# Two more feature groups through the seven-product scheme, early block products, fewer transposes on the matrix engine, and the last rows sent directly

## The chip, the cores and the metric

The kernel runs on one core of a Trainium2 chip. A core has five engines with their own instruction queues: PE (matrix products into PSUM, eight banks of 128 x 512 f32), DVE and ACT (both read PSUM; DVE adds, ACT applies functions such as Mish), POOL and SP. POOL, SP and ACT also issue DMAs, which all share the core's 16 DMA engines. Every queue is in order: an instruction that waits holds up what stands behind it on its engine.

The metric is the device time of one execution in microseconds (us). Three runs of the kernel before gave 936.93, 937.04 and 938.18, a median of 937.04.

## The reference

The network has four layers over `x` of 2048 tokens by 1024 channels (bf16), A B A B, each added to its input:

```
def _A_ref(x, w_r, w_i):
    X = rfft2(x.astype(float32)) * (w_r + 1j * w_i)
    return irfft2(X, s=(S, D)).astype(bfloat16)

def _B_ref(x, w1, b1, w2):
    h = einsum("bsd,df->bsf", x, w1) + b1
    act = h * tanh(softplus(h))               # Mish
    return einsum("bsf,fd->bsd", act, w2)

x = x + _A_ref(_layernorm(x), ...)
x = x + _B_ref(_layernorm(x), ...)            # and both once more
```

`w1` is 1024 x 3584 and `w2` 3584 x 1024. Both A layers use the same filter, both B layers the same weights.

## The kernel before, in words

**Layer A** computes the transforms as matrix products in stages (`s1`, `s2`, `s3`, the filter, `i1`, `i2`, `i4`). `s1` reads a rearranged copy `XR` of the normalized rows. For the second A layer `XR` is filled from the end of the first B layer, as described below.

**Layer B** works on 2048 tokens as two passes of 1024, each pass as two chunks of 512 tokens. The normalized rows of chunk c are held transposed in `XT[c]`, eight blocks of 128 channels by 512 tokens. The 3584 features are 14 groups of 256 (two tiles of 128).

For a pass, the first product `x w1` can be done in two ways for each feature group:

- *plain* (`mm1`, L1134): for each chunk, 2 feature tiles x 8 matrix products, so 32 products of 128x128 by 128x512 for the group. A chunk's product needs nothing of the other chunk. Three PSUM banks rotate; ACT applies Mish straight from PSUM.
- *seven products* (`quads`, L1178): Strassen's scheme in Winograd's form over a 2 x 2 split (two feature tiles and two halves of the channels on the side of the weights; two halves of the channels and two chunks on the side of the tokens). A group takes 7 products of 4 matrix products each, 28 in all, with sums of weight blocks (S1 to S4, four POOL instructions per group, L1081, on the first use; afterwards they are read back from a scratch tensor in DRAM) and sums of token blocks (T1 to T4 on DVE, L1163: three by the first call of `token_sums`, T3 by the second, which overwrites a part of `XT` and so comes after the last plain product of chunk 1). The block product A11·B11 is copied out of PSUM by ACT (L574) as P1, because several outputs need it, and the bank is then also accumulated further by A12·B21. DVE adds the parts (L1191, five per group), and ACT applies Mish.

In the order before, in each layer's first pass, groups 0 to 5 are plain and 6 to 13 go through the seven products. In the second pass all 14 do. The first pass of each layer begins under a filling-up phase: the last product of layer A (`i4`, called from `rest`), the residuals, the layernorm statistics (four tiles' sums on ACT, L453) and the transposes of chunk 1 run while PE does plain products of chunk 0. Its order on PE is: groups 0 to 3 of chunk 0 in halves, groups 4 and 5 of chunk 0 with the transposes of chunk 1's first two tiles inside group 5, then chunk 1 (groups 0 and 1 in halves, with the other two transposed tiles inside, then 2 to 5), then `quads`. The order on ACT around groups 4 and 5 is: Mish of group 2, two statistics instructions of tile 6 (L453), Mish of group 3, two of tile 7, then Mish of groups 4 and 5. The weight sums of the first four seven-product groups wait on POOL for a gate, namely the DVE instruction that normalizes tile 7. All weight loads go out through SP.

`products` (L1276) is the second product with `w2`, also in a seven-product scheme, with seven stages n of four token tiles t; `extra(n, t)` is other work put between. In pass 1's `products`, tiles 12 to 15 of the next pass are normalized at (1, 3). Tile 12 is turned by 8 DMA transposes issued one by one from SP (`normal`, `turn`), tiles 13 to 15 by 8 PE transposes each at (2, 2) with an ACT copy out of PSUM (`transposed`, L1100).

In the last `products` of the first B layer, each finished tile j is normalized and brought into `XR`, as rows: tiles up to 14 by a store to a DRAM scratch (`xn_store`, POOL) and a load from it one step later (`xr_load`, SP), tile 15 by 16 direct transfers from its buffer (`xr_direct`, 16 KB each, over POOL, ACT and SP). PE meanwhile repeats 24 products whose result nobody reads (`spin`, L650), and then waits for `XR`.

Of the kernel before, what the change touches and what calls it, by code (L numbers as in the profile page):

```python
# [180 lines left out]
class KB:  # L181
# [513 lines left out]
    def layer_A(self, li):  # L695
# [254 lines left out]
        self.w1_buf = [self.alloc(f"W1_{i}", (self.ob["WS"] + i * 4096, 140 * K)[i > 4], [8, 256]) for i in range(6)]  # L950
        for fg in range(6):
            self.load_w1(self.w1_buf[fg].ap, fg, [self.w1_buf[fg].res], after=self.r_ut)
# [118 lines left out]
    def fill_slot(self, b, fg, after=()):  # L1071
# [5 lines left out]
        self.load_w1(b.raw, fg, [b.res])  # L1077
        A = lambda n: self.wblock(b, n)
# [6 lines left out]
    def layer_B(self, li, last):  # L1085
# [92 lines left out]
        def quads(fgs, slot_of, B, after, lead=None):  # L1178

            sums = open_sums()  # L1180

            def product(n, bank, a, b, start):
# [5 lines left out]
                            for db in range(4)], reads=[s.res, s.rs] + list(res), writes=[self.r_bank[bank]])  # L1188
# [9 lines left out]

            def parts(n):
                a, b, d = (3 * (n % 2) + i for i in range(3))  # L1200
                return a, b, d, sums[n % 2], sums[2 + n % 2], sums[4], 2 * fgs[n]

            N = len(fgs)
            for n in range(N + 1):
                if n < N:
                    a, b, d, p1, u2, u3, ft = parts(n)
                    product(n, a, "A11", "B11", True)
                    self.copy(act, p1.ap, PS[:, a, :], [self.r_bank[a]], [p1.res])
                    product(n, b, "S2", "T2", True)
                    add(u2, b, p1)  # L1210
                if n == N and lead:
                    lead()
                if n:
                    _, pb, pd, q1, q2, q3, pft = parts(n - 1)
                    mish(1, pft + 1, q3.ap, q3.res)
                    product(n - 1, pb, "A22", "T4", False)
                    add(q1, pb, q1)
                    mish(0, pft + 1, q1.ap, q1.res)
                    product(n - 1, pd, "S4", "B22", False)
                    add(q2, pd, q2)  # L1220
                    mish(1, pft, q2.ap, q2.res)
                    after(n - 1)
                if n < N:
                    product(n, d, "S1", "T1", True)
                    product(n, a, "A12", "B21", False)
                    mish(0, ft, PS[:, a, :], self.r_bank[a])
                    product(n, b, "S3", "T3", False)
                    add(u3, b, p1)
                    add(u3, d, u3)
# [203 lines left out]
        assert self.u0 == P  # L1433
        for j in range(4, 8):
            residual(j)
# [9 lines left out]
        mm1(0, 4)  # L1445
        at_tiles(1)
        mm1(0, 5, mid=turns(1, 0, 1))
# [6 lines left out]
        early = self.open_slots("WE", self.ob["W2"], 0, 1, 2, 3)  # L1454
        for n in range(4):
            self.fill_slot(early[n], 6 + n, [gate])
# [9 lines left out]
        ws = []  # L1466
        for fg in range(2, 6):
            if fg in (2, 4, 5):
                ws += self.open_slots("WS", self.ob["WS"], len(ws))
                self.fill_slot(ws[-1], 9 + len(ws))  # L1470
            mm1(1, fg)
            if fg == 2:
                token_sums(0, last=False)
            if fg == 3:
                for j in range(8, 12):
                    residual(j)
        order = early + ws + early[:1]
        B = token_sums(0)
        self.xn_buf = self.xn_out + [self.alloc(f"XN{i}", self.ob["XN2"] + i * 2048, [self.D]) for i in range(2)]

        def after(n):
            if n == 0:
                self.fill_slot(order[7], 13)
            if 1 <= n < 4:
                load_b(STD, n // 3, (n - 1) % 2)
            if n < 4:
                self.stats_dve(8 + n)
            if n == 4:
                self.scales(8, 4)
            if n > 3:  # L1490
# [158 lines left out]
```

## Time and profile before

| what | value |
|---|---|
| median of three runs | 937.04 us |
| the profiled execution, its own time | 936.66 us |
| its span, first to last instruction | 934.9 us |
| PE busy | 875.9 us, 94% of the span |
| DVE, ACT, POOL busy | 619.1, 427.5, 159.0 us |
| mean granted PE clock | 0.987 |
| `mm1` (L1148) | 576 matrix products |
| `quads` (L1186) | 1232 matrix products |
| `products` (L1268) | 1568 matrix products |

PE is busy nearly everywhere, but a busy PE is modelled and a matrix product's duration (379 ns for 512 columns) contains a latency that overlaps with the next one. What one more product costs is read from a run of them without a wait: in the chain of work, 216 products of L1186 take 46.62 us, so 0.2158 us each; a product of 256 columns takes 0.109 us (16 in 1.75 us), a 128-column transpose 0.056 us (24 in 1.34 us).

### The profile page before, as it was taken

The numbers are of one execution on the slowest core, as the hardware profiler recorded it, in microseconds if no ns is written. First come the engines' busy times: TensorE is split into PE (matmuls) and PEld (weight loads), VectorE is DVE, ScalarE is ACT, GpSimd is POOL, SyncE is SP. The second block draws the span as 40 slices with busy tenths as digits, with TensorE's granted clock in tenths as the row PEclk, the third lists the DMA queues.
The fourth block names the chain that finished last, engine by engine and source line by source line (L and its number), as shares of the span: only waits on it lengthen the run. The fifth ranks groups of instructions, "written<-read, shape, count | busy, mean of one in ns | idle before, by whom it ended". The sixth has DMA issues, their size and how long they took to land.

```text
span 934.9 us, 13481 instructions
## 1 busy us (share of the span) xinstructions
PE 875.9 (94%) x5473; PEld 471.7 (50%) x5473; DVE 619.1 (66%) x973; ACT 427.5 (46%) x623; POOL 159.0 (17%) x183
## 2 busy tenths in 40 slices
PE   0799799999999999999979987999999999999998
PEld 0577486444444444444437765754444444444443
DVE  7698468686889667568746865647746665554473
ACT  7798485456203485510008975745551015552000
POOL 4922004950005642000130200000000000000000
PEclk9999999999999999999999997999999999999999
DMA  9969854676895488274640797433255635832432
GB/s 288 265 227 300 204 151 131 216 249 171 268 274 196 164 314 296 91 261 142 241 133 32 227 228 196 158 118 119 54 190 175 207 113 193 279 118 78 171 127 110
DMA packets 146335, 174.68 MB, mean 187 GB/s; under 512 B 66248, under 2 KB 125736, under 8 KB 146152
## 3 DMA queue, kind: packets, MB, share of 16 engines
q1 hardware_dynamic: 133424, 127.48, 44.5%
q0 software_dynamic: 10672, 44.67, 13.4%
q10 hardware_dynamic: 2176, 1.66, 0.6%
q8 instruction: 43, 0.70, 0.3%
q14 instruction: 20, 0.16, 0.0%
HBM read 130.00 MB, written 40.89 MB: 183 GB/s over the span
## 4 chain that ended last, share of the span: by engine, by line
PE 83%; DMA 5%; DVE 5%; ACT 2%; SPq 2%; POOL 1%; issue 1%; DVEq 0%; ACTq 0%; POOLq 0%
PE PS L1268 35%; PE PS L1186 28%; PE PS L1148 9%; SPq L251 2%; PE PS L799 2%; PE PS L725 2%; PE PS L824 2%; PE PS L1020 2%; POOL ARENA L1081 1%; PE PS L1109 1%; DMA ARENA<-in_A_x_dram 1%; DMA ARENA<-c_bt 1%; DMA ARENA<-u_scratch 1%; DMA u_scratch<-ARENA 1%; PE PS L635 1%; ACT ARENA L641 1%
## 5 line engine op out<-in xcount | busy, mean ns | idle before, releaser
L1268 PE MATMUL PS<-ARENA 128*128 128x512 bf16 x1568 | 340.1, 379 | 0.0
L1186 PE MATMUL PS<-ARENA 128*128 128x512 f16 (+1 forms) x1232 | 267.8, 379 | 0.4 <-POOL ARENA L1081 0.3
L1268 PEld LDWEIGHTS PS<-ARENA 128*128 128x128 bf16 x1568 | 153.4, 98 | 184.5
L1191 DVE TENSOR_TENSOR ARENA<-PS,ARENA 128x512 f32<-128x512 f32 x220 | 151.7, 691 | 95.7 <-PE PS L1186 90.7
L1186 PEld LDWEIGHTS PS<-ARENA 128*128 128x128 bf16 x1232 | 120.1, 98 | 146.8 <-POOL ARENA L1081 2.2
L1196 ACT ACTIVATE ARENA<-ARENA,B 128x512 bf16<-128x512 f32 x132 | 95.1, 721 | 66.5 <-DVE ARENA L1191 60.6
L574 ACT ACTIVATE ARENA<-PS 128x512 f32<-128x512 f32 (+2 forms) x82 | 61.1, 745 | 119.1 <-PE PS L1186 96.4
L1148 PE MATMUL PS<-ARENA 128*128 128x256 bf16 (+1 forms) x576 | 86.7, 308 | 0.3
L1081 POOL TENSOR_TENSOR ARENA<-ARENA 128x512 bf16<-128x512 bf16 x56 | 71.4, 1274 | 72.6 <-DVE ARENA L524 58.3
L453 ACT ACTIVATE ARENA<-XS 128x1024 bf16<-128x1024 bf16 x52 | 54.8, 1053 | 36.5 <-DVE XS L1319 33.0
L1148 PEld LDWEIGHTS PS<-ARENA 128*128 128x128 bf16 x576 | 55.2, 98 | 26.7 <-DVE ARENA L1114 1.0
L1293 DVE TENSOR_TENSOR ARENA<-ARENA 128x3584 bf16<-128x3584 bf16 x32 | 63.9, 2018 | 0.0
L1319 DVE TENSOR_TENSOR XS<-PS,ARENA 128x512 bf16<-128x512 f32 x52 | 35.7, 690 | 38.9 <-PE PS L1268 38.7
L1152 ACT ACTIVATE ARENA<-PS,B 128x256 bf16<-128x256 f32 (+1 forms) x72 | 38.3, 542 | 35.3 <-PE PS L1148 34.8
L1311 DVE TENSOR_TENSOR ARENA<-PS,ARENA 128x512 f32<-128x512 f32 x48 | 32.9, 688 | 28.9 <-PE PS L1268 28.4
L1196 ACT ACTIVATE ARENA<-PS,B 128x512 bf16<-128x512 f32 x44 | 30.2, 686 | 18.0 <-PE PS L1186 18.0
L1307 DVE TENSOR_TENSOR ARENA<-ARENA,XS 128x512 f32<-128x512 f32 x52 | 36.7, 731 | 0.5
L1163 DVE TENSOR_TENSOR ARENA<-ARENA 128x2048 f16<-128x2048 bf16 x16 | 25.3, 1582 | 17.6 <-PE PS L1148 17.3
L799 PE MATMUL PS<-ARENA 128*128 128x256 bf16 x256 | 32.4, 273 | 3.9 <-DVE ARENA L788 3.2
L472 DVE BATCH_NORM_STATS2 BN<-XS 128x6 f32<-128x512 bf16 x52 | 32.6, 669 | 4.5 <-DMA XS<-in_A_x_dram 4.5
L444 ACT ACTIVATE RS<-MV,EPS 128x1 f32<-128x1 f32 (+2 forms) x11 | 3.3, 296 | 70.7 <-DVE MV L565 70.0
L777 ACT ACTIVATE ARENA<-PS 128x1024 bf16<-128x1024 f32 x32 | 33.3, 1071 | 4.5 <-PE PS L773 4.5
(97 smaller groups left out, 820.9 us busy)
## 6 DMA issues: line engine op xcount, KB each, us to landing
ARENA<-in_B_w_dram SPq DMA_DIRECT2D x30, 896.0 KB, 6.4
ARENA<-w1s_scratch SPq DMA_DIRECT2D x30, 896.0 KB, 4.7
ARENA<-w2s_scratch SPq DMA_DIRECT2D x24, 896.0 KB, 6.7
ARENA<-in_B_w_dram SPq DMA_DIRECT2D x26, 512.0 KB, 5.2
w1s_scratch<-ARENA POOLq DMA_DIRECT2D x14, 896.0 KB, 4.2
u_scratch<-ARENA SPq DMA_DIRECT2D x14, 512.0 KB, 3.5
ARENA<-u_scratch SPq DMA_DIRECT2D x14, 512.0 KB, 5.9
w2s_scratch<-ARENA POOLq DMA_DIRECT2D x8, 896.0 KB, 4.1
```

Of the source, the lines that this page charges most:

```text
L453: self.op(act, lambda e, i=i, f=f: e.activation(junk.ap, x, f, accum_out=sums[:, i:i + 1]), reads=[self.r_xs[j]], writes=[junk.res], parts ...
L574: fn = (lambda e: e.activation(dst, src, ACT.Copy)) if scale is None else \
L799: fns.append(lambda e, c=c, part=part: e.matmul(ps[:, c * 256:(c + 1) * 256], yk.ap[:, part, c * P:(c + 1) * P], t[:, (128, 0)[part]:(384, ...
L1081: self.op(self.pool, lambda e, dst=A(dst), x=A(x), y=A(y), op=op: e.tensor_tensor(dst, x, y, op), reads=[b.res] + list(after), writes=[b.rs])
L1148: fns.append(lambda e, db=db, bank=bank, fl=fl: e.matmul(PS[:, bank, 0:w], wb.ap[:, db, fl * P:(fl + 1) * P], x.ap[:, db, tok], start=(db ...
L1152: self.op(act, lambda e, bank=bank, ft=ft, at=at: e.activation(at[:, tok], PS[:, bank, 0:w], ACT.Mish, bias=self.B1[:, ft:ft + 1]), reads= ...
L1186: self.group([lambda e, db=db: e.matmul(PS[:, bank, :], A[:, db, :], mov[:, db, :], start=(start and db == 0), stop=(db == 3), skip_group_ ...
L1191: self.op(dve, lambda e: e.tensor_tensor(dst.ap, PS[:, bank, :], x.ap, ALU.add), reads=[self.r_bank[bank], x.res], writes=[dst.res])
L1196: self.op(act, lambda e: e.activation(at, src, ACT.Mish, bias=self.B1[:, ft:ft + 1]), reads=[res, self.r_b1], writes=[ra])
L1268: self.group([lambda e, i=i, k=k, b=PB[n][k].ap: e.matmul(PS[:, bank, :], ap[:, i, t * P:(t + 1) * P], b[:, i - 7 * k, :], start=(start an ...
L1293: self.op(dve, lambda e: e.tensor_tensor(ap[dst][:, f, :], ap[x][:, f, :], ap[y][:, f, :], op), reads=part(x, k) + part(y, k), writes=part ...
L1307: self.op(dve, lambda e: e.tensor_tensor(a[t], a[t], x, ALU.add), reads=[rx], writes=[r[t]])
```

## The change

Six things change; the first four are in the first pass of each B layer.

1. Groups 4 and 5 move from plain to the seven products: plain are 0 to 3, and `quads` runs over ten groups, 4 to 13. Only four plain weight buffers remain.
2. `quads` is split. `first(n)` does the two products of group n that read chunk 0 only (A11·B11 with the ACT copy of P1, then A12·B21 with its Mish). It is called for the first four groups where plain groups 4 and 5 of chunk 0 stood: three times before the transposes of chunk 1's first two tiles, once after. `run` then leaves these two products out for the first four groups. Two more P1 buffers are given, so that four stand at once.
3. The loads of those groups' raw weights (`fill_raw`) are issued earlier than their sums (`fill_sums`), and a product waits for the sums only if it reads one. The gate stays where it was.
4. The loads, statistics, scales and normalizations that `after(n)` issues are moved to other values of n; two more slots are refilled within the run.
5. At (1, 3) of the first `products`, tiles 12 and 13 (in the last layer 12, 13 and 14) go by DMA transposes, and only 14 and 15 (15) by PE.
6. At the end of the first B layer, tiles 13 and 14 go by `xr_direct` too (8 transfers each, alternating between POOL and SP; tile 12 is loaded in the step of tile 13), tile 15's 16 transfers are dealt out to ACT, POOL, SP as 6, 6 and 4, and `spin` repeats 38 products instead of 24.

The core of the diff:

```
-        for fg in range(6):
+        for fg in range(4):
             self.load_w1(self.w1_buf[fg].ap, fg, ...)
...
+    def fill_raw(self, b, fg):
+        r = self.r_w1d[fg]
+        if r.writes:
+            self.dma(self.sp, b.ap[:, 0:2048], self.w1s_d[fg][:, 0:2048], ..., writes=[b.res])
+        else:
+            self.load_w1(b.raw, fg, [b.res])
...
-                            for db in range(4)], reads=[s.res, s.rs] + list(res), ...
+                            for db in range(4)], reads=[s.res] + [s.rs] * (a[0] == "S") + list(res), ...
...
+            def block(n):
+                a, b, d, p1, u2, u3, ft = parts(n)
+                product(n, a, "A11", "B11", True)
+                self.copy(act, p1.ap, PS[:, a, :], [self.r_bank[a]], [p1.res])
+            def corner(n):
+                a, b, d, p1, u2, u3, ft = parts(n)
+                product(n, a, "A12", "B21", False)
+                mish(0, ft, PS[:, a, :], self.r_bank[a])
+            def first(n):
+                block(n)
+                corner(n)
...
-        mm1(0, 4)
         at_tiles(1)
-        mm1(0, 5, mid=turns(1, 0, 1))
+        first, run = quads(list(range(4, 14)), order, B, (102 * 1024, self.ob["XN2"]))
+        for n in range(3):
+            first(n)
+        for f in turns(1, 0, 1):
+            f()
+        first(3)
...
-        for fg in range(2, 6):
+        for fg in (2, 3, 4, 5):
...
-                normal(12)
-                for j in (13, 14, 15):
+                for j in range(12, by_pe):
+                    normal(j)
+                for j in range(by_pe, 16):
                     xn[j] = self.apply(j)
...
-                if j < 15:
+                if j < 13:
                     self.xn_store(j, b)
-                if j > 8:
-                    self.xr_load(j - 1)
-                if j == 15:
-                    self.xr_direct(j, b, 2, (pool, act, sp))
+                    if j > 8:
+                        self.xr_load(j - 1)
+                elif j < 15:
+                    self.xr_direct(j, b, 1, (pool, sp))
+                    if j == 13:
+                        self.xr_load(12)
+                else:
+                    self.xr_direct(j, b, 2, (act, pool, sp, act, pool, act, pool, sp) * 2)
...
-            self.spin(24, 7)
+            self.spin(38, 7)
```

## The prediction

> **What bounds the kernel now.** I read the page first: PE is busy for 94% of the span, so I looked for where PE would wait afterwards. The chain of waits, in the first layer B (columns: start, length, what, all us), shows PE running without a hole through the place that is rebuilt:
>
> ```profile
> 137.08 10.42 PE PS L1148 x72
> 147.50 0.89 PE PS L1109 x16
> 148.39 4.35 PE PS L1148 x32
> 153.22 1.30 DVE ARENA L1114 x2
> 154.57 17.48 PE PS L1148 x96
> 172.05 46.62 PE PS L1186 x216
> ...
> 481.85 6.10 DMA ARENA<-ARENA
> 488.19 5.29 PE PS L635 x48
> ```
>
> So every product taken away is worth its 0.216 us (46.62 / 216), and every new wait on PE costs its full length. The last two lines are the hand-over to the second layer A: there a direct row transfer ends the wait.
>
> The timeline of the other engines around it tells what PE will wait for:
>
> ```profile
> 143.21 0.82 ACT L1152 ACTIVATE ARENA<-PS,B 128x256 bf16<-128x256 f32 x2
> 145.10 1.06 ACT L453 ACTIVATE ARENA<-XS 128x1024 bf16<-128x1024 bf16 x1
> 146.15 2.08 ACT L1152 ACTIVATE ARENA<-PS,B 128x512 bf16<-128x512 f32 x3
> 154.55 5.55 DVE L1163 TENSOR_TENSOR ARENA<-ARENA 128x2048 f16<-128x2048 bf16 x3
> 160.03 6.32 DVE L1396 TENSOR_TENSOR XS<-XS,ARENA 128x1024 bf16<-128x1024 bf16 x4
> 166.68 4.85 POOL L1081 TENSOR_TENSOR ARENA<-ARENA 128x512 bf16<-128x512 bf16 x4
> 172.16 2.50 DVE L1163 TENSOR_TENSOR ARENA<-ARENA 128x2048 f16<-128x2048 bf16 x1 [5.82 <-PE PS L1148]
> 172.95 0.60 ACT L574 ACTIVATE ARENA<-PS 128x512 f32<-128x512 f32 x1 [0.17 <-PE PS L1186]
> ```
>
> ACT is late here: group 4's Mish, ready on PE at about 144, begins at 146.15, after tile 7's statistics (L453). DVE has 5.82 us to spare before T3, the last L1163.
>
> **The change part by part** (durations from the one profiled execution, 936.66 us with a span of 934.9; the median shown is 0.38 above it).
>
> *Fewer products.* Two groups go from 32 to 28 products in each layer: 16 x 0.216 = -3.45 us.
>
> *The early products wait for ACT.* Before, PE filled three banks in turn and went on while ACT lagged. Now A12·B21 goes into the bank that ACT must first have copied as P1, directly behind A11·B11 and with nothing between them. Group 4's A11·B11 takes bank 0, whose last Mish (group 3) ends at 144.03; so it ends at about 145.0. Its copy stands behind tile 7's statistics and runs from 146.15 to 146.75. From ACT to PE I take 0.15 us (the last L641 copy ends at 500.03, L725 starts at 500.18), so A12·B21 ends at 147.76. Each further group costs 0.86 + 0.04 + 0.60 + 0.15 + 0.86 = 2.51 us instead of 1.73; Mish of the one runs under the A11·B11 of the next. Groups 5 and 6 end at 152.8, the transposes (1.00 with their gap) at 153.8, group 7 at 156.3. Before, the same point was 148.39 + 8 x 0.216 = 150.12: +6.2 us. DVE's scales and normalizations hang on the transposes and move with them, and so do the next transposes; only 0.1 of PE's 0.34 us wait ahead of 154.57 is absorbed: +6.1 us in each layer, +12.2 in all. With no hand-over time it would be +5.5 a layer; those are the bounds 11.0 and 12.4.
>
> *Raw weights.* Landings before: 141.3 for the first, 143.1 for the second, and the transfers' burst ends by 147. Needed are they at 144.1, 147.8, 150.3 and 153.8. Nothing; if the cover were gone, the wait would be one landing, 5 us.
>
> *T3 comes too late in the first layer.* DVE does T1, T2, T4 (5.55 us), four residuals (6.32) and T3 (2.50) in a row, 14.4 us from 154.55. PE, with plain groups 4 and 5 of chunk 1 gone, starts `run` 10.4 us after 154.57 (32 products of 256 columns at 0.109 and 32 of 512) and needs T3 after two products, at 12.1. Then DVE must add u2 first (0.69) before S3·T3 may enter that bank: 14.4 + 0.7 - 12.1 = 2.9 us of wait. In the second layer POOL is idle and the same rows are short (3.74, 2.49, 1.23 us); T3 waits for the plain product itself, and 0.3 is left. Sum +3.2 (bounds 0.5 and 3.9: a T3 as short as the second layer's, or one that waits another hand-over of every kind).
>
> *POOL's sums.* They follow the gate, which moves by 5 us. A group takes 4.86 + 0.87 = 5.73 us on POOL (5.9 to 6.6 beside DVE's work). From 157.5 on, groups 5 to 10 are ready at 170.6, 177, 183, 188.6, 194.3, 200.1. PE, starting at 171.1 and held by T3, asks for them at 176.5, 181, 185, 190, 196, 202. Nothing, with only 2 us to spare; the wait for T3 is the cover. In the second pass two fewer groups are summed there, and A11·B11 need not wait for sums: the 0.34 us wait at 311.0 goes, -0.3.
>
> *DVE, ACT and slots in the run.* The first four groups take 4.3 us of PE each, five DVE adds 3.5, three Mishes on ACT 2.2; statistics (1.5) come from the third on. It fits; uncovered, one statistics pair would cost PE 0.5. The four sums' loads of the second layer are four more SP issues, ahead of nothing that is due within 10 us. Refills of slots are needed over 12 us after they are issued.
>
> *Transposes.* 24 fewer on PE: 8 in the first layer, 16 in the second, 24 x 0.056 = -1.34. Of the 24 tile blocks each now stands on SP's queue as a DMA transpose at 1.27 us (16 took 20.38), two per step of 3 us, done by stage 4; T sums at (5, 3) are 12 us later, and the weight loads behind them had as much. Nothing; uncovered, 8 of them would cost 10 us.
>
> *The hand-over.* SP's direct transfers of tile 15 started at 481.27, since SP was held by the load of tile 14, which waits for its store (476.99 + 3.62). Now SP holds no load at that time; of tiles 13 and 14 it and POOL issue four pieces each, 2.6 and 2.2 us (0.64 and 0.54 apiece) in steps of 3.02, and SP tile 12's load, whose store lands by 475.5. Tile 15 is normalized at 479.35 as before; the first half's last issue is the third of ACT or POOL, about 480.8 (ACT 0.70, POOL 0.54 apiece). Landings of 16 KB took 2.1 to 6.1 us, so 483 to 487; `spin` ends at 476.5 + 8.2 = 484.7 at the earliest. I take a start of 485.7 against 488.19, -2.5 (bounds -3.4 and -1.1). Further, the clock: before, PE idle from 481.7 to 488.2 came back at half clock, visible in the windows (last columns PEclk, DMA, GB/s):
>
> ```profile
> 486.50:487.00 0.50, 0.00 (x0) 0.00 (x0) 0.00 (x0) 0.00 (x0) 0.00 (x0) 0.56 0.22 62
> 493.00:493.50 0.50, 0.50 (x9) 0.50 (x7) 0.50 (x1) 0.00 (x0) 0.00 (x0) 0.62 0.00 0
> ...
> 567.00:568.00 1.00, 0.31 (x13) 0.34 (x14) 0.00 (x0) 0.00 (x0) 0.00 (x0) 1.00 0.64 144
> 568.00:568.50 0.50, 0.50 (x26) 0.50 (x22) 0.00 (x0) 0.00 (x0) 0.00 (x0) 0.98 0.64 144
> 568.50:569.00 0.50, 0.15 (x6) 0.04 (x2) 0.00 (x0) 0.32 (x1) 0.00 (x0) 0.50 0.64 142
> ```
>
> With 1 us of idling it stays up. `s1` then is bound by its 16 copies (ACT 1.02 to 0.93, DVE 1.23), which end 9.9 us after its start instead of 11.99: -2.0 (bounds 0 and -2.4). Together -4.5.
>
> [...]
>
> *The clock in the new holes.* PE now idles about 1.9 us twice at 142 to 147 and, in the first layer, 2.9 at T3. The lines at 566 to 568.5 show the clock halved after only 1.7 us of idling with little around it. A halved stretch lasted 6.7 to 10.1 us. At half clock an early group takes 4.25 us rather than 2.51, so a stretch costs 2.7 at least; bounds 0 and 3 places x 2.7 = 8. I take half of one, +1.4. [...]
>
> Sum: -3.45 + 12.2 + 3.2 - 0.3 - 1.34 - 4.5 + 1.4 = +7.2; 936.66 + 7.2 = 943.9. I say **944.0**.
>
> **The rivals.**
>
> - *The waits fall into slack* (faster). Place: 142 to 156, price 12.2. For it: DVE and POOL have idle time there; against it: PE has none. If the holes cost below 2.6 us a layer instead of 6.1, the change gains; with none, 936.66 - 6.4 = 930.3 (no clock loss). Chance 0.06.
> - *They are partly hidden* (half of the early waits and of T3): about 936 to 939. Chance 0.08.
> - *The clock falls in several of the holes*: without the clock's term the sum is 942.5, and 2 or 3 x 2.7 make it 948 to 950.5. For it the lines at 568; against it those at 554 to 558, with PE busy by half and the clock up. Chance 0.15.
> - *The direct rows do not come earlier*: POOL and SP now carry 16 more issues, and tile 15's transfers could stand behind tile 14's. Without the 4.5: 948.4. For it the landings of 6.1; against it the DMA engines, 0.14 to 0.65 busy in most of those us. Chance 0.13.
> - *POOL becomes the bound of the first layer's run*: were every group to take 7.4 us as the first does (6.57 + 0.87), group 9's sums would come at 201 for 196: +5, 949. Chance 0.06.
>
> **How the numbers follow.** The forecast's own case, 941 to 946.5, has a chance of 0.52. The range 939.5 to 949.5 leaves out the faster case, the partly hidden one and the upper end of the clock case. About 0.2% (1.9 us) is what a measurement tells from no change. Faster: 0.06 and a small share of the partly hidden, 0.07; the same: 0.07; slower: 0.86.
>
> **What would show it.** In the profile after, PE waits at the early products' line for ACT's L574, once about 1.9 us and three times 0.7 to 0.8 in each layer, and once about 2.9 us for DVE's first add behind T3, in the first layer only. The first product of the run comes 10.4 us after the second pair of transposed tiles. The 128-column transposes fall by 24, `spin` runs to 484.7 after shifting, L635 starts within 1.5 us of it at full clock, and `s1` takes 10 us. I am wrong if ACT's copy of P1 does not hold PE, or if the hand-over gains much more than 5 us.

## The result, and the profile after

The changed kernel takes 963.56 us (median of four runs, 960.72 to 964.71) beside 937.61 for the kernel before: a ratio of 1.0272, with a 95% interval from 1.0246 to 1.0298. The forecast was 944.0 with a range up to 949.5; the sign was right, and the size too small by a factor of nearly four. The profiled execution took 964.36 us with a span of 962.6, against 936.66 and 934.9: 27.7 us more (26.0 between the medians).

Both programs go through the same stages on PE, so the difference can be laid out by the start of each stage's first product (from the timeline of PE in both traces; the last column is what the forecast's terms make of it):

| stage on PE, us | before | after | difference | forecast |
|---|---|---|---|---|
| start to the last `i4` of the first layer pair | 136.92 | 139.25 | +2.3 | 0 |
| from there to chunk 1's first product, first pair | 13.04 | 20.93 | +7.9 | +6.1 (and the clock, 1.4 in all) |
| on to `products` (rest of the plain groups, the run) | 68.55 | 75.72 | +7.2 | +1.2 |
| `products` of the first pass | 87.67 | 92.42 | +4.8 | -0.4 |
| seven-product groups of the second pass | 83.86 | 82.96 | -0.9 | -0.3 |
| last `products`, hand-over, up to `s1` | 98.15 | 98.70 | +0.5 | -2.5 |
| `s1` to `i4` of the second pair | 79.50 | 78.70 | -0.8 | -2.0 |
| second pair: to chunk 1's first product | 13.04 | 20.90 | +7.9 | +6.1 |
| second pair: on to `products` | 68.55 | 67.55 | -1.0 | -1.4 |
| second pair: `products` of the first pass | 87.68 | 87.56 | -0.1 | -0.9 |

The three stages that are left out (the second pair's last `i4`, second pass and last `products`) add up to 0.0. In the first row the two kernels differ in weight loads alone. In the 14 executions profiled for this study this point was reached between 136.9 and 140.4 us, and the six of them that keep the old form of the first layer up to there span that whole range; so the 2.3 lie within the variation from one execution to the next.

Who waited for whom on PE in the changed kernel (total us, times, longest):

```profile
PE PS L1208 <- ACT ARENA L574: 7.5, 8, 1.7
PE PS L1208 <- DVE ARENA L1213: 5.3, 3, 3.1
PE PS L635 <- DMA ARENA<-ARENA: 4.0, 1, 4.0
PE PS L1208 <- ACT ARENA L1173: 4.0, 2, 2.0
PE PS L1307 <- DMA ARENA<-in_B_w_dram: 3.3, 1, 3.3
PE PS L1307 <- DMA ARENA<-w2s_scratch: 0.6, 1, 0.6
```

L1208 is `quads` now, L1307 `products`. Before, L1186 waited 0.3 us in all and L1268 not at all. Five lines are new: 11.5 us for ACT, 5.3 for DVE, 3.9 for the second matrix's loads; and the hand-over's wait is 4.0 instead of 6.5, after a `spin` that is 3 us longer.

The early products in the first layer, on PE's timeline (start, length, what, and in brackets the idle time ahead):

```profile
146.64 0.81 PE L1208 MATMUL PS<-ARENA 128*128 128x512 bf16 x3 [1.99 <-ACT ARENA L1173]
149.12 3.43 PE L1208 MATMUL PS<-ARENA 128*128 128x512 bf16 x8 [1.66 <-ACT ARENA L574]
153.23 1.90 PE L1208 MATMUL PS<-ARENA 128*128 128x512 bf16 x8 [0.69 <-ACT ARENA L574]
155.82 1.04 PE L1208 MATMUL PS<-ARENA 128*128 128x512 bf16 x4 [0.69 <-ACT ARENA L574]
...
159.31 1.04 PE L1208 MATMUL PS<-ARENA 128*128 128x512 bf16 x4 [0.69 <-ACT ARENA L574]
160.18 2.78 PE L1169 MATMUL PS<-ARENA 128*128 128x256 bf16 x24
```

The waits are the forecast's, one of 1.99, one of 1.66 and three of 0.69. What the forecast sized too small is in the second line: eight products take 3.43 us there and 1.90 in the line below. The windows of the same place (busy time of each engine, then PEclk, DMA share, GB/s) show why:

```profile
148.00:149.00 1.00, 0.00 (x0) 0.00 (x0) 0.87 (x2) 1.00 (x3) 0.00 (x0) 1.00 0.17 51
149.00:150.00 1.00, 0.89 (x3) 0.42 (x4) 0.00 (x0) 0.06 (x1) 0.00 (x0) 0.66 0.00 0
150.00:151.00 1.00, 1.00 (x3) 0.30 (x2) 0.00 (x0) 0.13 (x1) 0.00 (x0) 0.50 0.00 0
152.00:153.00 1.00, 0.54 (x2) 0.00 (x0) 0.00 (x0) 0.42 (x1) 0.00 (x0) 0.63 0.00 0
153.00:154.00 1.00, 0.77 (x4) 0.41 (x5) 0.00 (x0) 0.18 (x1) 0.00 (x0) 1.00 0.00 0
```

After two holes of under 2 us the granted clock is halved, although PE was busy with a few products between them, and it stays so for 3.4 us. The same windows show four more such stretches that the trace of before does not have at these places, 3.4 us each: from 180 us (behind the wait for T3), 224 (behind a wait at the scales), 302 (behind the wait for loads), and 624 (the second pair's early products). At half clock a product takes about twice as long, as the 3.43 and 1.90 us for eight show, so I estimate that each stretch costs half its length: five times 1.7 = 8.5 us.

The next three waits on PE's timeline, in the run and in `products` of the first layer:

```profile
180.18 41.68 PE L1208 MATMUL PS<-ARENA 128*128 128x512 f16 x180 [3.08 <-DVE ARENA L1213]
```

```profile
223.85 8.34 PE L1208 MATMUL PS<-ARENA 128*128 128x512 f16 x30 [1.99 <-DVE ARENA L1213]
```

```profile
302.38 26.11 PE L1307 MATMUL PS<-ARENA 128*128 128x512 bf16 x110 [3.26 <-DMA ARENA<-in_B_w_dram]
```

The first was forecast (2.9). The second comes from DVE, where the scales of tiles 8 to 11 now meet POOL's last sums:

```profile
218.19 0.52 DVE L502 TENSOR_SCALAR RS<-MV 128x4 f32<-128x4 f32 x1
218.94 1.00 DVE L513 TENSOR_TENSOR RS<-RS 128x4 f32<-128x4 f32 x1
219.98 0.16 DVE L514 TENSOR_TENSOR RS<-RS 128x4 f32<-128x4 f32 x1
220.17 1.00 DVE L515 SCALAR_TENSOR_TENSOR RS<-RS 128x4 f32<-128x4 f32 x1
...
222.64 0.55 DVE L524 TENSOR_SCALAR FD<-XS,MV,RS 128x1024 bf16<-128x1024 bf16 x1
```

Operations on 128 x 4 numbers take up to 1.00 us here, while POOL's last sums run from 217.50 to 222.39; before, each of the same lines took 0.16 or 0.17 (204.64 to 206.22, POOL's last sum having ended by 201.4). The third wait is SP's queue:

```profile
271.51 11.91 SPq L250 DMA_TRANSPOSE ARENA<-ARENA  x8
283.52 1.13 SPq L251 DMA_DIRECT2D ARENA<-in_B_w_dram  x2
284.71 12.63 SPq L250 DMA_TRANSPOSE ARENA<-ARENA  x8
297.45 1.12 SPq L251 DMA_DIRECT2D ARENA<-in_B_w_dram  x2
```

The last line is the issue of the sixth stage's two loads (B22). They stand behind the 8 DMA transposes of tile 13 and the rest of tile 12's; before, the first of them was issued at 269.35, 50.8 us after `products` began, now 61.6 us after.

At the hand-over, the queue of SP and the end of the chain of waits:

```profile
495.62 0.60 SPq L251 DMA_DIRECT2D ARENA<-xn_scratch  x1
496.28 3.26 SPq L251 DMA_DIRECT2D ARENA<-ARENA  x4
499.58 0.66 SPq L251 DMA_DIRECT2D ARENA<-xn_scratch  x1
500.61 4.98 SPq L251 DMA_DIRECT2D ARENA<-ARENA  x8
```

```profile
503.71 6.03 DMA ARENA<-ARENA
509.98 5.37 PE PS L635 x64
```

SP waits for the store of tile 11 until 495.62 before it can load it, then issues its four pieces of tile 13 in 3.26 us (0.6 us each but the last, which takes 1.38), the load of tile 12, and only then four pieces each of tiles 14 and 15, until 505.6. The piece that releases PE was issued at 503.71 and took 6.03 us to land.

### The profile page after: what moved, and what is told of

Same layout as the page of the kernel before. It is cut to its first block, busy times and chain, and to the rows that moved or that the text cites. A ratio compares the mean times of both kernels' runs of the same rounds, so it can differ in the third digit from the quotient of the medians.

```text
span 962.6 us, 13420 instructions
## 1 busy us (share of the span) xinstructions
PE 879.4 (91%) x5372; PEld 470.2 (49%) x5447; DVE 631.2 (66%) x993; ACT 427.7 (44%) x624; POOL 160.2 (17%) x189
## 4 chain that ended last, share of the span: by engine, by line
PE 77%; DVE 8%; DMA 6%; ACT 5%; SPq 4%; issue 1%; POOL 0%; ACTq 0%; DVEq 0%
PE PS L1307 32%; PE PS L1208 29%; PE PS L1169 4%; SPq L251 3%; PE PS L799 2%; PE PS L725 2%; PE PS L1020 2%; PE PS L824 2%; ACT ARENA L453 1%; DMA ARENA<-in_A_x_dram 1%; SPq L250 1%; PE PS L1130 1%; DVE ARENA L1184 1%; DMA ARENA<-c_bt 1%; DMA ARENA<-u_scratch 1%
## 5 line engine op out<-in xcount | busy, mean ns | idle before, releaser
L1307 PE MATMUL PS<-ARENA 128*128 128x512 bf16 x1536 | 340.5, 380 | 5.6 <-DMA ARENA<-in_B_w_dram 3.3
L1208 PE MATMUL PS<-ARENA 128*128 128x512 f16 (+1 forms) x1318 | 299.1, 385 | 18.0 <-ACT ARENA L574 7.5
L1307 PEld LDWEIGHTS PS<-ARENA 128*128 128x128 bf16 x1568 | 153.5, 98 | 190.4 <-issue 5.5
L1213 DVE TENSOR_TENSOR ARENA<-PS,ARENA 128x512 f32<-128x512 f32 x240 | 164.0, 690 | 99.0 <-PE PS L1208 93.6
L1208 PEld LDWEIGHTS PS<-ARENA 128*128 128x128 bf16 x1344 | 131.2, 99 | 183.3 <-ACT ARENA L574 12.0
L1218 ACT ACTIVATE ARENA<-ARENA,B 128x512 bf16<-128x512 f32 x144 | 103.5, 721 | 89.1 <-DVE ARENA L1213 83.4
L574 ACT ACTIVATE ARENA<-PS 128x512 f32<-128x512 f32 (+2 forms) x86 | 63.4, 737 | 124.5 <-PE PS L1208 101.7
L1169 PE MATMUL PS<-ARENA 128*128 128x256 bf16 (+1 forms) x446 | 59.8, 290 | 0.2
L1350 DVE TENSOR_TENSOR ARENA<-PS,ARENA 128x512 f32<-128x512 f32 x48 | 32.9, 687 | 27.9 <-PE PS L1307 27.5
L1218 ACT ACTIVATE ARENA<-PS,B 128x512 bf16<-128x512 f32 x48 | 32.9, 686 | 24.6 <-PE PS L1208 24.6
L1173 ACT ACTIVATE ARENA<-PS,B 128x256 bf16<-128x256 f32 (+1 forms) x56 | 27.6, 501 | 23.3 <-PE PS L1169 23.0
L781 DVE TENSOR_TENSOR ARENA<-ARENA 128x1024 bf16<-128x1024 bf16 x32 | 22.0, 688 | 19.5 <-ACT ARENA L777 19.5
```

What stands on the lines that cost most here:

```text
L574: fn = (lambda e: e.activation(dst, src, ACT.Copy)) if scale is None else \
L1169: fns.append(lambda e, db=db, bank=bank, fl=fl: e.matmul(PS[:, bank, 0:w], wb.ap[:, db, fl * P:(fl + 1) * P], x.ap[:, db, tok], start=(db ...
L1208: self.group([lambda e, db=db: e.matmul(PS[:, bank, :], A[:, db, :], mov[:, db, :], start=(start and db == 0), stop=(db == 3), skip_group_ ...
L1213: self.op(dve, lambda e: e.tensor_tensor(dst.ap, PS[:, bank, :], x.ap, ALU.add), reads=[self.r_bank[bank], x.res], writes=[dst.res])
L1218: self.op(act, lambda e: e.activation(at, src, ACT.Mish, bias=self.B1[:, ft:ft + 1]), reads=[res, self.r_b1], writes=[ra])
L1307: self.group([lambda e, i=i, k=k, b=PB[n][k].ap: e.matmul(PS[:, bank, :], ap[:, i, t * P:(t + 1) * P], b[:, i - 7 * k, :], start=(start an ...
```

## The experiments

All ratios are to the kernel before, measured beside it, with 95% intervals. The expectations call PE TensorE, DVE VectorE, ACT ScalarE and POOL GpSimd.

**Clock: fill the holes.** Throwaway products on a bank that nothing reads are put where PE waits:

```
             def first(n):
+                if n == 0:
+                    self.spin(8, 5)
                 block(n)
+                self.spin(3 if n else 7, 5)
                 corner(n)
...
                         if n >= ready:
                             corner(n)
+                        if ready and n == 0 and not last:
+                            self.spin(13, 7)
                         product(n, b, "S3", "T3", False)
```

> The changed kernel with throwaway products on a bank that nothing reads put into three holes of TensorE: the waits for ScalarE among the early products (both layers), and the wait for T3 in the first layer's run. The waits themselves stay as long as they are. Theory (each hole costs about 1.7 us again, since the trace's clock is halved for 3.41 us after a hole of only 1.7 to 2 us): three half-clock stretches go, 963.6 - 5.1 = about 958.5. Rival (the stretches at half clock hide in the following waits and cost nothing): no change, 963.6; if the throwaway products delay the real ones, up to 3 us more.

Measured: 960.14 us, ratio 1.0238 [1.0217, 1.0259], against 1.0272 [1.0246, 1.0298] for the change.

```profile
146.81 1.67 PE L652 MATMUL PS<-BD 128*128 128x512 bf16 x7
148.64 1.90 PE L1208 MATMUL PS<-ARENA 128*128 128x512 bf16 x8 [0.15 <-ACT ARENA L574]
150.38 0.81 PE L652 MATMUL PS<-BD 128*128 128x512 bf16 x3
151.23 1.90 PE L1208 MATMUL PS<-ARENA 128*128 128x512 bf16 x8
```

L652 is `spin`. The eight products now take 1.90 us at once, the clock stands at 1.00 through 146 to 153 and again behind T3. The early stage falls from 20.9 to 19.4 in both pairs, 3.0 us, as the theory had it. The run falls from 60.7 to 58.5, but not by the filled hole alone: the wait at the scales grew from 1.99 to 2.94, and the stretch at half clock behind it is gone although nothing was put there. That the sum, 5.3 us, meets the theory's 5.1 is therefore in part luck; the last section comes back to this hole. Half of the gain was given back at the next wait: SP's loads were not earlier, their wait grew from 3.3 to 4.8, and the half clock behind it from 3.4 to 6.8 us (`products` 92.4 to 95.2). The intervals of the two ratios overlap, so it is the stages and the lines above, and not the total, that carry this experiment.

**Early products: another order.**

```
                 a, b, d = (3 * (n % 2) + i for i in range(3))
+                if n < ready:
+                    a, b = b, a
...
-            if fg > 1:
-                self.stats_act(4 + fg)
+            if fg == 2:
+                self.stats_act(6)
...
-        for n in range(3):
-            first(n)
+        for n in range(2):
+            block(n)
+        for n in range(2):
+            corner(n)
+        block(2)
         for f in turns(1, 0, 1):
             f()
-        first(3)
+        block(3)
+        for n in range(2, 4):
+            corner(n)
+        self.stats_dve(7)
-        self.sums_to_mv(6, 2)
+        self.sums_to_mv(6, 1)
```

> The changed kernel with another order of the early products (two blocks, two corners, one block, turns, one block, two corners), even groups taking the bank that comes free first, and tile 7's statistics on VectorE, which stands idle there, instead of ScalarE. Theory (the 6.1 us per layer are ScalarE's latency and backlog, not its rate: it is busy 1.3 us per 1.7 us of products): waits on ScalarE among the early products fall to 0.5 to 1 us per layer and the half-clock stretch goes; the stage from the end of the last stage of the mixer to the second chunk's first products falls from 20.9 to about 14 us, twice 7 us, 963.6 - 14 = about 949.6; up to 3 us may come back as a longer wait for the second matrix's halves. Rival (ScalarE's rate bounds the stage): it stays above 18 us, 958 or more.

Measured: 948.26 us, 1.0097 [1.0072, 1.0123]. The second pair:

```profile
611.40 1.89 PE L1208 MATMUL PS<-ARENA 128*128 128x512 bf16 x8
613.81 2.85 PE L1208 MATMUL PS<-ARENA 128*128 128x512 bf16 x12 [0.52 <-ACT ARENA L574]
616.50 1.06 PE L1130 MATMUL PS<-IDENT,ARENA 128*128 128x128 bf16 x16
617.40 2.75 PE L1208 MATMUL PS<-ARENA 128*128 128x512 bf16 x12
620.16 2.78 PE L1169 MATMUL PS<-ARENA 128*128 128x256 bf16 x24
```

One wait of 0.52 is left, and no stretch at half clock. The stage takes 14.3 and 14.0 us instead of 20.9; before it was 13.0. So the early waits were ACT's latency between two products in one bank, and its backlog, and they cost with their clock 6.6 and 6.9 us. The two were repaired together, so how they share it is not shown. What is left in the first pair is a wait of 0.86 us for a load of raw weights, which the forecast had as covered. The scales' wait in the first layer's run grew to 3.81 (from 1.99) and that for the loads is 3.55 (from 3.26): those are causes of their own.

**DVE beside POOL.** The sums on POOL are left out in the first pass of the first layer, and a transfer fills their place:

```
-        for dst, x, y, op in (("S1", ...), ("S3", ...), ("S2", ...), ("S4", ...)):
-            self.op(self.pool, lambda e, ...: e.tensor_tensor(dst, x, y, op), ...)
+        self.dma(self.sp, b.ap[:, 2048:3584]..., self.w1...[:, 0:6, fg * 256:(fg + 1) * 256], ...)
```

> The changed kernel with the four weight sums of each group left out on GpSimd in the first pass of the first layer; the place of the sums is filled with first-matrix weights by a transfer, so the products have their operands and the same count, and the result is wrong for that. Theory (VectorE is slowed by GpSimd working on the same memory): with the sums gone residuals 8 to 11 take 2.5 us instead of 6.3 and T3's wait falls to the 0.3 us of the second layer, the scales' operations to 0.16 us, the run from 60.7 to about 53: 963.6 - 7.5 = about 956. Rival (the order on VectorE alone makes T3 late): its wait stays near 3 us.

Measured: 952.71 us, 1.0149 [1.0129, 1.0169]. DVE, from residuals 8 to 11 on (L1432), with T3 (L1181) and two of the scales' lines:

```profile
170.47 2.49 DVE L1432 TENSOR_TENSOR XS<-XS,ARENA 128x1024 bf16<-128x1024 bf16 x4
177.51 1.22 DVE L1181 TENSOR_TENSOR ARENA<-ARENA 128x2048 f16<-128x2048 bf16 x1 [4.55 <-PE PS L1166]
...
216.76 0.16 DVE L513 TENSOR_TENSOR RS<-RS 128x4 f32<-128x4 f32 x1
216.96 0.16 DVE L514 TENSOR_TENSOR RS<-RS 128x4 f32<-128x4 f32 x1
```

Residuals 8 to 11 take 2.49 us instead of 6.81, T3 1.22 instead of 2.17, the scales' operations 0.16, T3's wait on PE is 0.27, and the run takes 52.52 as in the second pair. POOL's sums are what makes DVE late at both places. The wait for loads shrank with it, to 0.55 and 0.85 us (`products` 88.9): the two loads go out 58.8 us after `products` began instead of 61.6. The transposes do not begin earlier relative to `products` (11.2 us ahead of it, 12.7 in the changed kernel), but SP gets through them faster, the last eight in 10.39 us for 12.63; why is open. The total would be lower still, but the early stage took 24.6 us in both pairs this time: the same waits were followed by 13.7 us at half clock instead of 3.4.

**T3 and the scales moved.** In the first layer alone:

```
-                for j in range(8, 12):
+                for j in range(8, 10 if li == 0 else 12):
                     residual(j)
...
         def after(n):
+            if li == 0 and n < 2:
+                residual(10 + n)
...
-            if n == 6:
+            if n == (6 if li else 8):
                 self.scales(8, 4)
-            if n > 5:
-                normal(2 + n)
-                turn(4)
+            for j in ({6: (8,), 7: (9,), 8: (10,), 9: (11,)} if li else {8: (8, 9), 9: (10, 11)}).get(n, ()):
+                normal(j)
+            if n > (5 if li else 7):
+                turn(4 if li else 8)
```

> The changed kernel with two edits in the first layer alone: residuals 10 and 11 go behind T3 on VectorE, into the first two groups of the run, and the scales of tiles 8 to 11 come after group 8, when GpSimd's sums are done, instead of after group 6. Theory (T3 is late because four residuals stand before it while GpSimd's sums slow them to 1.6 us each; the scales' small operations take 1.0 us where they meet a sum): the 3.1 us wait falls below 0.7, the waits of 1 to 2 us at the scales go, with their two half-clock stretches; the run falls from 60.7 to about 53.5: 963.6 - 7 = about 956.5. The later transposes on SP may lengthen the 3.3 us wait for the second matrix's halves, up to 4 us: 960.5. Rival (T3 itself is what the sums slow): the wait stays over 2 us and the run over 57.

Measured: 971.17 us, 1.0334 [1.0299, 1.037], slower than the change itself. The run behaves as expected, 53.4 us, with 1.1 us of wait for T3 and none at the scales. But in `products`:

```profile
259.22 3.17 PE L1307 MATMUL PS<-ARENA 128*128 128x512 bf16 x7 [11.55 <-DMA ARENA<-in_B_w_dram]
```

SP's transposes begin 0.9 us after `products` instead of 12.7 before it, and a load that is due at 247.7 lands 11.5 us late; 13.7 us at half clock follow, and `products` takes 102.3. My 4 us for that were far too few. The early stage was 24.7 us again, with 13.7 us at half clock in each pair.

**Which part holds up the loads.** Three kernels. Part 5 alone on the kernel before (tiles 13, and 14 in the second pair, by DMA):

```
+        by_pe = 15 if last else 14
...
-                normal(12)
-                for j in (13, 14, 15):
+                for j in range(12, by_pe):
+                    normal(j)
+                for j in range(by_pe, 16):
                     xn[j] = self.apply(j)
```

> The kernel before with part 5 alone: tile 13 of the first layer, tiles 13 and 14 of the second are turned by 8 DMA transposes each on SP instead of on TensorE. Forecast: -1.34 us (936.3), since SP has time. Theory now (the loads of the second matrix's halves stand behind the added transposes): the first layer's products wait 3.3 us for them, with a half-clock stretch of 1.7 us, and the second layer's 0.6: 937.6 - 1.3 + 5.6 = about 941.9. Rival (loads are late only together with the schedule two groups later): 936.3.

Measured: 940.63 us, 1.0037 [1.0013, 1.006]. `products` of the first pass take 92.0 us there instead of 87.7, with this wait on PE:

```profile
286.29 2.06 PE L1268 MATMUL PS<-ARENA 128*128 128x512 bf16 x7 [2.59 <-DMA ARENA<-in_B_w_dram]
288.89 23.78 PE L1268 MATMUL PS<-ARENA 128*128 128x512 bf16 x103 [0.54 <-DMA ARENA<-in_B_w_dram]
```

In the second pair they take 87.9, so nothing is won there either. The changed kernel without parts 5 and 6 (the diff of both taken back):

> The changed kernel with its parts 5 (tiles 13 and 14 turned by DMA) and 6 (the last rows of the first layer) put back to the old form; the four feature groups, the early products and the later schedule stay. Theory (the 3.26 us wait of the first layer's products for the second matrix's halves comes from the added DMA transposes on SP's queue): that wait and its half-clock stretch go (-3.26 and -1.7), the 0.61 us one of the second layer too, the 24 transposes come back on TensorE (+1.34), the hand-over hardly moves: 963.6 - 5.6 + 1.3 = about 959.4. Rival (the loads are late because statistics and transposes of tiles 8 to 11 were moved two groups later): the wait stays and only the 1.34 us come back, about 965. Second rival (the direct rows gain at the hand-over what they were meant to): about 4 us more than either.

Measured: 962.27 us, 1.0262 [1.0226, 1.0298]. `products` are back at 87.67 and the loads' wait is gone, as the first theory said. The total did not show it: 0.9 us went back at the hand-over, where the short `spin` left 7.1 us of idling and 10.2 us at half clock, and the untouched first stage took 1.2 more. Last, the change with the two loads on POOL's queue:

```
-                PB[5][:] = [load_w2("B22", k, f"R{k + 1}") for k in range(2)]
+                PB[5][:] = [load_w2("B22", k, f"R{k + 1}", pool if li == 0 else sp) for k in range(2)]
```

> The changed kernel with one edit: the two loads of the second matrix that the sixth stage of the first layer's products waits for are issued by GpSimd's queue instead of SP's; the DMA transposes stay on SP. Theory (the loads wait for their turn behind transposes on SP's queue): the 3.3 us wait goes with its half-clock stretch, the first layer's products fall from 92.4 to about 87.4: 963.6 - 5 = about 958.6. Rival (the loads wait until their place in memory is free): the wait stays.

Measured: 957.09 us, 1.0203 [1.0182, 1.0225]. `products` take 88.4. On POOL the second load waits for PE, which frees its place, until 285.44, and goes out there: 52.6 us after `products` began, 9 us before SP came to it. The loads had waited for their turn on SP. The total holds other differences too: in this run the wait at the scales is 0.81 us instead of 1.99, and 6.8 us at half clock instead of 3.4 follow T3.

**The hand-over.** Part 6 alone on the kernel before:

> The kernel before with part 6 alone: rows of tiles 13 to 15 of the first layer go from chip memory to chip memory in many small pieces, and the throwaway products are 38 instead of 24. The forecast said -4.5 (937.6 - 4.5 = 933.1): rows ready 2.5 us earlier, 2.0 us by the clock. Theory now (more small pieces stand in line on the issuing engines and land 4 to 6 us later, so the last one is no earlier): first product of the second layer within 1 us of its old place, and 0.5 to 1 us gained by the clock: 936.5 to 938.5.

Measured: 938.11 us, 0.9999 [0.9984, 1.0014]: nothing. The old rows with 52 throwaway products:

```
-            self.spin(24, 7)
+            self.spin(52, 7)
```

> The kernel before with 52 throwaway products at the hand-over instead of 24. Theory (the clock is lost in the idle time after the throwaway products, and 6.8 us at half clock follow at the next layer's start): the stretch at half clock after the hand-over goes or shrinks to 3.4 us, the first stage of the second layer is 1 to 2 us shorter, 937.6 - 1.5 = about 936. Rival (the throwaway products still run when the rows land and delay the stage, or the clock is not what the stage costs): 937.6 or more.

Measured: 936.23 us, 0.9982 [0.997, 0.9994]. Part 6 with 50 of them:

> The kernel before with part 6 and 50 throwaway products instead of 38. Theory (part 6 leaves the rows no earlier; what can be had at the hand-over is the clock): as with the old rows and 52 throwaway products, 936.2, give or take 0.7. Rival (rows do land earlier by the 2.5 us that the forecast took, hidden so far by the half-clock stretch): 934 or less; the other way, if the throwaway products now outlast the rows: over 937.

Measured: 936.34 us, 0.9978 [0.9967, 0.9989], the same. The start of `s1` with part 6 alone and with the longer `spin` alone:

```profile
480.22 8.37 PE L652 MATMUL PS<-BD 128*128 128x512 bf16 x37
491.62 7.81 PE L635 MATMUL PS<-M,ARENA 128*128 128x128 bf16 x104 [3.04 <-DMA ARENA<-ARENA]
```

```profile
477.60 11.39 PE L652 MATMUL PS<-BD 128*128 128x512 bf16 x52
489.19 6.83 PE L635 MATMUL PS<-M,ARENA 128*128 128x128 bf16 x104 [0.20 <-DMA ARENA<-ARENA]
```

The same 104 products take 7.81 and 6.83 us (8.85 before). From the first product of the second pass's `products` to that of `s1` it is 97.7 us with part 6, 97.9 with the longer `spin` and 97.8 with both, against 98.15. With one way of sending, this stretch differs as much from run to run: over all profiled executions it is 97.0 to 98.7 us with part 6 (eight) and 97.6 to 98.7 with the old rows (six). So no gain from the rows is shown, and the forecast's 2.5 us are not there. What can be had is the clock. `s1` to `i4` falls from 79.5 to 77.5 once PE is kept busy until the rows are there, with either way of sending them.

**All repairs at once, and a mixture.** The change with the early products repaired further (tiles 6 and 7 both on VectorE, a bank for S2·T2 that is free), the first layer's T3 and scales moved as above, the old turns, the old rows and 52 throwaway products:

> The changed kernel in both layers with the repaired early products (tiles 6 and 7 on VectorE, free bank first), T3 ahead of two residuals and the scales after GpSimd's sums in the first layer, tiles 13 to 15 turned on TensorE again, the old rows of the hand-over and 52 throwaway products. Theory: early stage about 14 us, run of the first layer 53.4, its products 87.7 plus up to 2 us of wait for the loads that stand behind transposes which start later: 935 to 938, level with before. Rival (GpSimd's ten sums bound the first layer's run, since nothing else delays it any more): the run takes 55 or more and the time is over 939.

Measured: 948.91 us, 1.0113 [1.0097, 1.0129]. The early stage (14.1 and 13.3) and the run (53.8) come out, so POOL's ten sums do not bound it. But an 11.3 us wait for loads comes in `products` (100.5) even with only tile 12 of that group turned by DMA, since the transposes of tiles 8 to 11 begin 0.9 us after `products` and hold the load up until 243.41. I expected 2 us there. The second is the kernel before with 52 throwaway products and the repaired change in the second pair only:

```
-        self.w1_buf = [self.alloc(...) for i in range(6)]
-        for fg in range(6):
+        self.w1_buf = [self.alloc(...) for i in range(4 if li else 6)]
+        for fg in range(4 if li else 6):
...
-            self.spin(24, 7)
+            self.spin(52, 7)
```

> The kernel before with 52 throwaway products at the hand-over, and in the second layer alone the changed form (four plain feature groups, early products in the repaired order, with tiles 6 and 7 both on VectorE for their statistics and the free bank taken first; tiles 13 and 14 turned by DMA); the first layer and its hand-over stay as they were. Theory (four groups pay where GpSimd has no sums to make and no load stands behind the transposes): second layer's feature-mixing part 1.2 us shorter than before, its products 0.7 shorter, the hand-over 1.9 as measured with 52 alone: 938.1 - 3.8 = about 934.3. Rival (the waits of the early products stay near 1 us and the gain of four groups is gone): 935.5 to 936.2, as with the throwaway products alone.

Measured: 934.72 us, 0.9963 [0.9949, 0.9977]. It beats both kernels. By stages: 2.0 us of it at the hand-over, 1.0 in the first pair's second pass (82.9 for 83.9, as A11·B11 no longer waits for sums), and 0.5 in the second pair up to `products`, where I had expected 1.2. Its 87.97 us of `products` show part 5 giving nothing, where I had expected 0.7.

## Why the prediction was wrong

- *Fewer products, -3.45.* Holds: the run of the second pair takes 52.53 us where the waits are small. The second pair's stage came out 0.4 less favourable than forecast: in its run PE loses 0.43 us at T3 instead of 0.3, and three times 0.09 behind DVE's adds.
- *The early products wait for ACT, +12.2.* Holds, in place, kind and length. Reordering removes it.
- *T3, +3.2.* Holds: 3.08 in the first layer, 0.26 of idle time in the second.
- *The clock in the new holes, +1.4: half of one stretch.* This is the largest term that failed. There were five stretches, an estimated 8.5 us; at three places throwaway products kept the clock up. The price per stretch was too high (2.7 us, from stretches of 6.7 us and more; these last 3.41 and cost an estimated 1.7) and their number far too low. The step took the holes as doubtful because its own lines disagreed: at 566 to 568.5 the clock was halved behind 1.7 us of idling, at 554 to 558 it stayed up with PE busy by half. It went by the length of a hole, and that does not sort them here: the clock fell behind holes of 1.66 and 1.99 us and stayed up behind one of 2.94 (holes filled, at the scales). What sorts them is how busy PE was over 3.41 us, 0.46 to 1.42 us where the clock fell and 1.86 and 2.03 at that hole (last section). The rival "the clock falls in several of the holes" names what happened, but it looked at the early products and T3 alone.
- *DVE, ACT and slots in the run: it fits.* Failed. The durations were taken from a trace in which POOL was done before the scales began; two more groups of sums reach beyond them. 2.0 us of wait and a stretch at half clock.
- *Transposes, -1.34, and nothing on SP.* The first half holds, the second failed. The step said that the weight loads behind had as much room as the T sums. They did not: the loads of the sixth stage came 3.26 us late in the first layer, with 1.7 us for the half clock, and those of the second layer 0.61 us late. Its own "uncovered, 8 of them would cost 10 us" was the right kind of warning, with no row looked up for the time at which the load is due.
- *The hand-over, -4.5.* Failed, by 4.3 in the profile (+0.5 and -0.8). The step assumed that SP holds no load at that time. In the trace after, the store of tile 11 takes 6.67 us to land, SP sits on that tile's load until 495.62, its four pieces of tile 13 take 3.26 us where I took 2.6, and the piece that releases PE goes out at 503.71, 6 us after `products` ended, and lands 6 us later. The rival "the direct rows do not come earlier" happened: 16 more pieces in place of two stores and two loads gained nothing that the runs show.
- *Second pass, -0.3.* -0.9 in the first pair: I counted one of four waits for sums (PE's weight loads wait 0.84, 0.50, 0.43 and 0.47 us there before).

The failed terms are 7.1 (clock), 2.0 (scales), 3.9 (loads) and 4.3 (hand-over), 17.3 us, less 0.6 in the second pass; 2.3 us lie in the first row of the table. With 0.4 us in the second pair's run and 0.6 in the first's, which I have not traced, this is the way from the forecast's +7.2 to +27.7 up to 0.5.

## What to carry to other kernels

On an engine that never waits, a reordering that puts two dependent steps back to back costs the other engine's latency every time (here three waits of 0.69 us in each pair behind ACT's copy, and with the order changed one of 0.52 us in both pairs together); interleave two groups before counting what the removed work is worth. For each in-order queue that gets more work, write down the latest time at which the first load behind it is due, not only whether the queue has idle time: here SP issued the first of them 61.6 us after `products` began, for 50.8 before, and PE waited 3.26 us. And where holes cannot be avoided, judge them by PE's busy share over a few microseconds and not by the length of the longest: here half clock followed a hole of 1.99 us at the scales and did not follow one of 2.94. Throwaway work in the holes at three places kept the clock at 1.00.

## What I had not expected of the hardware

The half clock came in multiples of 3.41 us: stretches of 3.4, 6.8, 10.2 and 13.7 us in these traces. The same code with the same waits (1.8 to 2.0, 1.66, three times 0.69) was followed by 3.4 us in the changed kernel and by 13.7 in two of the experiments, 3.7 us dearer in each pair. The places repeat with the same step: in each of the 14 traces all stretches after 100 us begin on one grid of 3.41 us (in the changed kernel at 115.19, 149.32 and 180.04, for example, ten and nine steps apart). I call a step of this grid a window. PE's busy time in the window that ends where the next clock begins:

| kernel and place | window, us | PE busy, of 3.41 us | clock after it |
|---|---|---|---|
| changed, early products, first pair | 145.91 to 149.32 | 1.02 | half |
| changed, T3 (hole of 3.08) | 176.63 to 180.04 | 0.46 | half |
| changed, scales (hole of 1.99) | 221.01 to 224.42 | 1.42 | half |
| changed, loads (hole of 3.26) | 299.51 to 302.92 | 0.54 | half |
| changed, early products, second pair | 620.36 to 623.78 | 0.81 | half |
| holes filled, scales (hole of 2.94) | 216.32 to 219.73 | 2.03 | full |
| the same hole, next window | 219.73 to 223.15 | 1.86 | full |

The hole of 2.94 us lies across two windows and costs no clock, the shorter one of 1.99 lies in one and does. Over all 14 traces, from 130 us on and without the second layer A, PE was busy for at most 0.42 of each of the 27 windows behind which the clock fell, and for at least 0.49 of each of the 2801 behind which it stayed up. From half the clock came back behind 22 windows that were busy for 0.79 or more, and it stayed at half behind 20 with 0.80 or less. In the second layer A, with its narrower products, the shares do not sort it as well: there the clock also fell behind windows that were busy for up to 0.74. The difference between one stretch and four goes with it too: at half clock the early products filled 3.22 us of the first window in the changed kernel, and 1.98, 2.72 and 2.73 of the first three in the experiment without sums, whose grid lies differently. All this is sorted after the fact, with modelled ends of the products; no run moved a hole across the grid and changed nothing else, so the cause is argued here and not shown.

DVE operations of 0.16 us take up to 1.00 while POOL adds, and residuals of 0.62 us take 1.70 (2.49 and 6.81 for four); with POOL's adds gone both are short again.
